# A depthwise-separable convolution on one core: short chunks that share a ring buffer at both ends, and a last supertile in two column parts

## The chip, the cores and the metric

The kernel runs on one core of one Trainium2 chip. The metric is the device time in microseconds (us) of one execution; smaller is better. An execution of some 580 us shows a profiled span of about 578: the profile's span is 1.7 to 2.0 us shorter than the time told for the same run. PE is the matrix engine, PEld its weight loads, DVE the vector engine, ACT the scalar engine, POOL the GpSimd engine and SP the engine that issues nearly all DMA here. A transfer's *landing* is the time from its issue to the last update of its semaphore. For the last store the trace has 16 of these updates, one for each of the 16 DMA engines' shares, and a tiny packet of 4 bytes at the end of each share. A run can start its main loop up to 1.7 us earlier or later, whatever the kernel, as is shown below; differences of a few tenths are therefore read from stretches inside the profiles and not from the times.

## The reference, cut to what matters

```python
# x: (1, 384, 384, 384) bf16, dw: (1, 1, 384), pw: (384, 384)
out = x * dw[0, 0]                         # rewritten: what its padding and loop come to for k = 1
return jnp.einsum('bhwc,cd->bhwd', out, pw)
```

With a 1x1 depthwise kernel the whole is one matrix product: 147,456 rows of 384 channels times a 384x384 weight that has `dw` folded in. Each byte of `x` is read once and each byte of the output written once, 113 MB either way.

## The kernel before

Rows are worked on in **supertiles** of 512. There are 288 of them, numbered 0 to 287. DVE transposes a supertile into `T`, PE multiplies it with the built weight `w_r` into one of two PSUM tiles, ACT empties PSUM into the output buffer `O` (an *eviction*), and SP loads and stores. Loads and stores move **chunks** of up to 10 supertiles, through three buffers of `X` and three of `O`. The chunks are short at both ends, so that the first work starts early and the last store is small.

```python
LMAX = 10
NX = 3
NO = 3

def _chunks(n_super: int):
    head, tail = [1, 1, 2, 2, 3, 4, 5], [7, 5, 4, 2, 1, 1]
    mid = n_super - sum(head) - sum(tail)
    return head + [LMAX] * (mid // LMAX) + tail
# ... cut
        def load_x(t):                       # one chunk, one whole buffer of the ring
            L = chunks[t]
            r = 512 * s0[t]
            src = xf[r : r + 512 * L, :].rearrange("(p s) c -> p (s c)", p=P)
            d = nc.sync.dma_start(Xs[t % NX][:, : 4 * L, :].rearrange("p s c -> p (s c)"), src)
            if t >= NX:
                je = s0[t - NX] + chunks[t - NX] - 1
                d._wait_ge(s_t[je % 2][1], je // 2 + 1)
            d.then_inc(s_x[t % NX], 16)
# ... cut: PE's warm-up matmuls on zeros and the building of w_r
        with nc.tensor.Fori(0, NS // 2, 1) as it:      # all 288 supertiles, two in a turn
            rv = nc.tensor.to_reg(it + 1)
            for s in range(2):
                supertile(s, rv)                       # 48 matmuls of 384 columns
# ... cut
            nq = 4
            if jj + 1 == NS:                           # the last supertile: DVE empties half
                nq = 2
                e = nc.vector.tensor_copy(Ov[:, nq:4, j, :], PS[s][:, nq:4, :D])
                e._wait_ge(s_pe, 2 * jj + 2)
                e.then_inc(s_d)
            a = nc.scalar.copy(Ov[:, 0:nq, j, :], PS[s][:, 0:nq, :D])
            # ... and each of SP and ACT stores its half of the last supertile
```

Of the kernel before, what the change touches and what calls it, by code (L numbers as in the profile page):

```python
# [7 lines left out]
BF16 = mybir.dt.bfloat16  # L8
F32 = mybir.dt.float32
U32 = mybir.dt.uint32  # L10
COPY = mybir.ActivationFunctionType.Copy

LMAX = 10
NX = 3
NO = 3


def _chunks(n_super: int):

    head, tail = [1, 1, 2, 2, 3, 4, 5], [7, 5, 4, 2, 1, 1]  # L20
    mid = n_super - sum(head) - sum(tail)
    assert mid > 0 and mid % LMAX == 0
    return head + [LMAX] * (mid // LMAX) + tail


@with_exitstack
def kernel(
# [4 lines left out]
    pw: bass.AP,  # L32
    out: bass.AP,
):




    nc = tc.nc
    P = nc.NUM_PARTITIONS  # L40
    B, H, W, C = x.shape
    assert dw.shape[0] == 1 and dw.shape[1] == 1, "only k=1 depthwise supported"
    D = pw.shape[1]
    N = B * H * W
    assert C == 384 and D == 384 and N % 1024 == 0
    NB = C // 64

    xf = x.rearrange("b h w c -> (b h w) c")
    of = out.rearrange("b h w d -> (b h w) d")

    NS = N // 512
    chunks = _chunks(NS)
    NT = len(chunks)
    s0 = [sum(chunks[:t]) for t in range(NT)]

    consts = ctx.enter_context(tc.tile_pool(name="consts", bufs=1))
    bufp = ctx.enter_context(tc.tile_pool(name="bufs", bufs=1))
# [6 lines left out]
    w_r = consts.tile([P, NB, 2, D], BF16, name="w_r")  # L64
# [2 lines left out]
    warm = consts.tile([P, 3], F32, name="warm")  # L67
    zero = consts.tile([P, D], BF16, name="zero")

    Xs = [bufp.tile([P, 4 * LMAX, C], BF16, name=f"X{i}") for i in range(NX)]  # L70
    Ts = [bufp.tile([P, NB, 256], BF16, name=f"T{i}") for i in range(2)]
    Os = [bufp.tile([P, 4 * LMAX * D], BF16, name=f"O{i}") for i in range(NO)]
    PS = [psum.tile([P, 4, 512], F32, name=f"ps{s}") for s in range(2)]

    s_x = [nc.alloc_semaphore(f"s_x{i}") for i in range(NX)]
    s_t = [[nc.alloc_semaphore(f"s_t{i}{h}") for h in range(2)] for i in range(2)]
    s_pe = nc.alloc_semaphore("s_pe")
    s_a = [nc.alloc_semaphore(f"s_a{i}") for i in range(2)]
    s_d = nc.alloc_semaphore("s_d")
    s_o = [nc.alloc_semaphore(f"s_o{i}") for i in range(NO)]  # L80
    s_dw = nc.alloc_semaphore("s_dw")
    s_pw = nc.alloc_semaphore("s_pw")
    s_df = nc.alloc_semaphore("s_df")
# [3 lines left out]
    s_wr = [nc.alloc_semaphore(f"s_wr{e}") for e in range(2)]  # L87
    s_seed = nc.alloc_semaphore("s_seed")
    s_zero = nc.alloc_semaphore("s_zero")
    s_last = nc.alloc_semaphore("s_last")  # L90

    with tc.tile_critical():  # L92
        def load_x(t):
            L = chunks[t]
            r = 512 * s0[t]
            src = xf[r : r + 512 * L, :].rearrange("(p s) c -> p (s c)", p=P)
            d = nc.sync.dma_start(Xs[t % NX][:, : 4 * L, :].rearrange("p s c -> p (s c)"), src)
            if t >= NX:
                je = s0[t - NX] + chunks[t - NX] - 1
                d._wait_ge(s_t[je % 2][1], je // 2 + 1)  # L100
            d.then_inc(s_x[t % NX], 16)

        def store(t):
            L = chunks[t]
            r = 512 * s0[t]
            je = s0[t] + L - 1
            dst = of[r : r + 512 * L, :].rearrange("(q p j) d -> p q (j d)", q=4, p=P)
            src = Os[t % NO][:, : 4 * L * D].rearrange("p (q e) -> p q e", q=4)
            nc.sync.wait_ge(s_a[je % 2], je // 2 + 2)
            nc.sync.dma_start(dst, src).then_inc(s_o[t % NO], 16)  # L110


        nc.scalar.dma_start(dw_n[:], dw.rearrange("a e (k p) -> p (a e k)", p=P)).then_inc(s_dw, 16)
        nc.sync.dma_start(pw_n[:], pw.rearrange("(k p) d -> p k d", p=P)).then_inc(s_pw, 16)
        for t in range(NX):
            load_x(t)
        for t in range(NT - 1):
            if t + NX < NT:
                load_x(t + NX)
            store(t)  # L120
        o_last = Os[(NT - 1) % NO][:, : 4 * D].rearrange("p (q e) -> p q e", q=4)
        of_last = of[N - 512 :, :].rearrange("(q p) d -> p q d", p=P)
        nc.sync.dma_start(of_last[:, 2:4], o_last[:, 2:4])._wait_ge(s_d, 1).then_inc(
            s_last, 16
        )
        for o in range(NO):
            nc.sync.wait_ge(s_o[o], 16 * len(range(o, NT - 1, NO)))
        nc.sync.wait_ge(s_last, 32)



# [8 lines left out]
        def supertile(s, rv):  # L140
            for b in range(NB):
                for par in range(2):
                    for q in range(4):
                        if par == 0 and q == 0 and b in (0, 3):
                            nc.tensor.wait_ge(s_t[s][b // 3], rv)
                        mm = nc.tensor.matmul(  # L146
                            PS[s][:, q, :D],
                            lhsT=Ts[s][32 * q : 32 * q + 32, b, par::2],
                            rhs=w_r[32 * q : 32 * q + 32, b, par, :],
                            start=(b == 0 and par == 0),  # L150
                            stop=(b == NB - 1 and par == 1),
                            tile_position=(32 * q, 0),
                        )
                        if b == 0 and par == 0 and q == 0:
                            mm._wait_ge(s_a[s], rv)
                        elif s == 0 and q == 0 and par == 0:
                            mm._wait_ge(*w_done[b])
                        if b in (2, 5) and par == 1 and q == 3:
                            mm.then_inc(s_pe)
# [3 lines left out]
        with nc.tensor.Fori(0, 6, 1) as _:  # L163
            for i in range(8):
                nc.tensor.matmul(  # L165
                    PS[0][:, i % 4, :D],
                    lhsT=zero[32 * (i % 4) : 32 * (i % 4) + 32, 0:P],
                    rhs=zero[32 * (i % 4) : 32 * (i % 4) + 32, :],
                    start=True,
                    stop=True,  # L170
                    tile_position=(32 * (i % 4), 0),
                )
        nc.tensor.wait_ge(s_sel, 1)
        for b in range(NB):
# [4 lines left out]
            for r in range(2):  # L179
                mm = nc.tensor.matmul(  # L180
                    PS[1][:, 2 * (b % 2) + r, :D],
                    lhsT=sel[:, 2 * (b % 2) + r, :],
                    rhs=w_n[:, b // 2, :],
                    start=True,
                    stop=True,
                )
            mm.then_inc(s_w)
        nc.tensor.wait_ge(*w_done[0])
        with nc.tensor.Fori(0, NS // 2, 1) as it:
            rv = nc.tensor.to_reg(it + 1)  # L190
            for s in range(2):
                supertile(s, rv)


        nc.gpsimd.memset(warm[:], 0.0).then_inc(s_seed)  # L195
# [11 lines left out]
        for s in range(2):  # L207
            c = nc.scalar.copy(warm[:, s + 1 : s + 2], warm[:, 0:1])  # L208
# [2 lines left out]
            c.then_inc(s_a[s])  # L211

        def transposes(t, j):
            jj = s0[t] + j
            L = chunks[t]
            s = jj % 2
            Xw = Xs[t % NX][:].bitcast(U32)[:, : 4 * L, :].rearrange("p (k l) c -> p k l c", l=L)
            Tw = Ts[s][:].bitcast(U32).rearrange("p b (i k) -> p b k i", k=4)
            for h in range(2):
                if h == 0 and j == 0:  # L220
                    nc.vector.wait_ge(s_x[t % NX], 16 * (t // NX + 1))
                ins = nc.vector.transpose(  # L222
                    out=Tw[:, 3 * h : 3 * h + 3],
                    in_=Xw[:, :, j, 96 * h : 96 * h + 96].rearrange("p k (b w) -> p b k w", w=32),
                )
                if jj >= 2:
                    ins._wait_ge(s_pe, 2 * (jj - 2) + h + 1)
                ins.then_inc(s_t[s][h])

        order = [(t, j) for t in range(NT) for j in range(chunks[t])]  # L230

        def w_out(b):
            e = w_eng[b]
# [9 lines left out]
        for k in (0, 2):  # L243
            i = nc.vector.tensor_scalar_mul(w_n[:, k, :], pw_n[:, k, :], dw_f[:, k : k + 1])  # L244
            i._wait_ge(s_df, 1)
            i.then_inc(s_wn[k])
        i = nc.scalar.activation(w_n[:, 1, :], pw_n[:, 1, :], COPY, scale=dw_f[:, 1:2])  # L247
        i._wait_ge(s_df, 1)
        i.then_inc(s_wn[1])
        transposes(*order[0])  # L250
        for b in range(NB):
            w_out(b)
        transposes(*order[1])

        for jj, (t, j) in enumerate(order):
            L = chunks[t]
            s = jj % 2
            Ov = Os[t % NO][:, : 4 * L * D].rearrange("p (q j d) -> p q j d", q=4, d=D)
            if j == 0 and t >= NO:
                nc.scalar.wait_ge(s_o[t % NO], 16 * (t // NO))  # L260
            nq = 4
            if jj + 1 == NS:
                nq = 2
                nc.vector.wait_ge(s_o[t % NO], 16 * (t // NO))
                e = nc.vector.tensor_copy(Ov[:, nq:4, j, :], PS[s][:, nq:4, :D])  # L265
                e._wait_ge(s_pe, 2 * jj + 2)
                e.then_inc(s_d)
            a = nc.scalar.copy(Ov[:, 0:nq, j, :], PS[s][:, 0:nq, :D])  # L268
            a._wait_ge(s_pe, 2 * jj + 2)
            a.then_inc(s_a[s])  # L270
            if jj + 2 < NS:
                transposes(*order[jj + 2])
        nc.scalar.dma_start(of_last[:, 0:2], o_last[:, 0:2])._wait_ge(s_a[(NS - 1) % 2], (NS - 1) // 2 + 2).then_inc(
            s_last, 16
        )


# [28 lines left out]
```

## Time and profile before

| | before |
|---|---|
| time, median of 4 runs | 579.64 us (579.41 to 579.90) |
| span of the profiled run | 577.7 us |
| first matmul of the main loop | 10.28 us |
| eviction of supertile 286 begins | 570.44 us |
| issue of the last store, and its landing | 573.37 us, 3.0 us later |

The first 3 of those runs, which the prediction was made from, have a median of 579.63 us. How to read it: between the first matmul and the eviction of supertile 286 lies the loop, 287 supertiles of 1.95 us bound by PE. What lies before it is the head, what lies after it the tail, 7.3 us from the eviction of supertile 286 to the end of the span. That eviction is a good place to cut, because nothing that the change does to the last supertile comes before it. The lines themselves stand in the prediction.

### The profile page before, as it was taken

To read this page: it belongs to the slowest core of one execution; us is meant where nothing else is said; L and a number is where in the kernel's file an instruction comes from. 1 tells how busy PE (TensorE), PEld (TensorE's weight loads), DVE (VectorE), ACT (ScalarE), POOL (GpSimd) and SP (SyncE) were. 2 spreads that over 40 slices of the span, in tenths; PEclk is the share of its full clock that TensorE was granted. 3 is DMA by queue.
4 is the path that set the end of the run, shared out by engine and by line. 5 is a ranking of instruction groups with operands and counts; after the bars stand their busy time and mean duration, and the time that the engine had idled before them with its cause. 6 is when DMAs were issued, how large, how long until landed. Compare 5 with 4: busy or idle time off the path is not lost.

```text
span 577.7 us, 29746 instructions
## 1 busy us (share of the span) xinstructions
PE 569.2 (99%) x13884; PEld 417.2 (72%) x13884; DVE 505.0 (87%) x581; ACT 419.4 (73%) x297; POOL 1.7 (0%) x8
## 2 busy tenths in 40 slices
PE   7999999999999999999999999999999999999996
PEld 3677777777777777777777777777777777777774
DVE  5788898888988889988889888898888898888984
ACT  4777777777777777777777777777777777777775
POOL 1000000000000000000000000000000000000000
PEclk9999999999999999999999999999999999999999
DMA  5999999999999999999999999999999999997987
GB/s 185 360 415 420 430 425 428 438 423 414 426 430 440 405 390 403 423 397 395 402 424 393 395 419 408 397 403 420 406 376 400 426 400 389 397 359 272 367 338 270
DMA packets 26362, 226.88 MB, mean 393 GB/s; under 512 B 1648, under 2 KB 5616, under 8 KB 22384
## 3 DMA queue, kind: packets, MB, share of 16 engines
q1 hardware_dynamic: 25680, 226.60, 97.3%
q10 hardware_dynamic: 672, 0.20, 0.1%
q14 instruction: 9, 0.07, 0.0%
q8 instruction: 1, 0.02, 0.0%
HBM read 113.54 MB, written 113.25 MB: 393 GB/s over the span
## 4 chain that ended last, share of the span: by engine, by line
PE 98%; DMA 1%; DVE 0%; issue 0%; ACT 0%; SPq 0%; DVEq 0%
PE ps L146 97%; DMA pw_n<-in_pw_dram 1%; PE ps L180 0%; DVE w_r L235 0%; DVE O L265 0%; ACT w_r L235 0%; DVE w_n L244 0%; SPq L301 0%; DVEq L241 0%; SPq L92 0%
## 5 line engine op out<-in xcount | busy, mean ns | idle before, releaser
L146 PE MATMUL ps<-w_r,T 32*128 32x384 bf16 x13824 | 562.0, 321 | 0.1
L222 DVE STREAM_TRANSPOSE T<-X 128x384 uint32<-128x384 uint32 x576 | 501.6, 875 | 58.8 <-PE ps L146 3.2
L268 ACT CAST O<-ps 128x1536 bf16<-128x1536 f32 x288 | 413.9, 1437 | 148.1 <-PE ps L146 148.1
L146 PEld LDWEIGHTS ps<-w_r,T 32*128 32x128 bf16 x13824 | 414.4, 93 | 147.6 <-issue 0.8
L244 DVE TENSOR_SCALAR w_n<-pw_n,dw_f 128x384 bf16<-128x384 bf16 x2 | 0.6, 318 | 5.6 <-DMA pw_n<-in_pw_dram 5.6
L165 PE MATMUL ps<-zero 32*128 32x384 bf16 x48 | 4.0, 520 | 1.4 <-POOL zero L196 1.4
L180 PE MATMUL ps<-w_n,sel 128*128 128x384 bf16 x12 | 3.3, 389 | 1.6 <-DVE w_n L244 0.6
L235 ACT CAST w_r<-ps 128x768 bf16<-128x768 f32 x4 | 3.1, 800 | 1.9 <-PE ps L180 1.9
L180 PEld LDWEIGHTS ps<-w_n,sel 128*128 128x128 bf16 x12 | 0.9, 106 | 4.3 <-issue 3.5
L165 PEld LDWEIGHTS ps<-zero 32*128 32x128 bf16 x48 | 1.9, 135 | 2.9 <-issue 1.7
L265 DVE CAST O<-ps 128x768 bf16<-128x768 f32 x1 | 1.0, 958 | 3.0 <-PE ps L146 3.0
L235 DVE CAST w_r<-ps 128x768 bf16<-128x768 f32 x2 | 1.9, 957 | 1.0 <-PE ps L180 1.0
L208 ACT ACT_TABLE_LOAD x1 | 1.3, 1283 | 1.5 <-SPq L92 1.5
L240 ACT CAST dw_f<-dw_n 128x3 f32<-128x3 bf16 x1 | 0.2, 192 | 2.0 <-DMA dw_n<-in_dw_dram 2.0
L247 ACT ACTIVATE w_n<-pw_n,dw_f 128x384 bf16<-128x384 bf16 x1 | 0.6, 615 | 0.4 <-DMA pw_n<-in_pw_dram 0.4
L198 POOL TENSOR_SCALAR_AFFINE_SELECT sel<-ones 128x512 bf16<-128x512 bf16 x1 | 0.7, 737 | 0.1
L197 POOL MEMSET ones<- 128x512 bf16 x1 | 0.5, 531 | 0.0
L208 ACT COPY warm<-warm 128x1 f32<-128x1 f32 x2 | 0.3, 188 | 0.0
L196 POOL MEMSET zero<- 128x192 uint32 x1 | 0.3, 258 | 0.0
L195 POOL MEMSET warm<- 128x3 f32 x1 | 0.1, 101 | 0.5 <-SPq L92 0.5
L290 POOL MEMSET const-bfloat16-1.0<- 128x1 bf16 x1 | 0.1, 102 | 0.0
L290 POOL MEMSET const-uint8-127<- 128x1 uint8 x1 | 0.1, 102 | 0.0
(2 smaller groups left out, 0.2 us busy)
## 6 DMA issues: line engine op xcount, KB each, us to landing
X<-in_x_dram SPq DMA_DIRECT2D x25, 3840.0 KB, 21.8
out_dram<-O SPq DMA_DIRECT2D x25, 3840.0 KB, 27.7
X<-in_x_dram SPq DMA_DIRECT2D x2, 1920.0 KB, 14.1
out_dram<-O SPq DMA_DIRECT2D x2, 1920.0 KB, 18.0
X<-in_x_dram SPq DMA_DIRECT2D x2, 1536.0 KB, 9.9
out_dram<-O SPq DMA_DIRECT2D x2, 1536.0 KB, 14.4
X<-in_x_dram SPq DMA_DIRECT2D x1, 2688.0 KB, 20.1
out_dram<-O SPq DMA_DIRECT2D x1, 2688.0 KB, 11.9
```

The costliest lines, as they stand in the source:

```text
L146: mm = nc.tensor.matmul(PS[s][:, q, :D], lhsT=Ts[s][32 * q : 32 * q + 32, b, par::2], rhs=w_r[32 * q : 32 * q + 32, b, par, :], start=(b = ...
L165: nc.tensor.matmul(PS[0][:, i % 4, :D], lhsT=zero[32 * (i % 4) : 32 * (i % 4) + 32, 0:P], rhs=zero[32 * (i % 4) : 32 * (i % 4) + 32, :], s ...
L180: mm = nc.tensor.matmul(PS[1][:, 2 * (b % 2) + r, :D], lhsT=sel[:, 2 * (b % 2) + r, :], rhs=w_n[:, b // 2, :], start=True, stop=True,)
L197: nc.gpsimd.memset(ones[:], 1.0).then_inc(s_seed)
L198: nc.gpsimd.affine_select(out=sel[:].rearrange("p (v r) (q w) -> p v r q w", v=2, q=4), in_=ones[:].rearrange("p (v r) (q w) -> p v r q w" ...
L208: c = nc.scalar.copy(warm[:, s + 1 : s + 2], warm[:, 0:1])
L222: ins = nc.vector.transpose(out=Tw[:, 3 * h : 3 * h + 3], in_=Xw[:, :, j, 96 * h : 96 * h + 96].rearrange("p k (b w) -> p b k w", w=32),)
L235: i = nc.vector.tensor_copy(out, in_) if e == 0 else nc.scalar.copy(out, in_)
L244: i = nc.vector.tensor_scalar_mul(w_n[:, k, :], pw_n[:, k, :], dw_f[:, k : k + 1])
L247: i = nc.scalar.activation(w_n[:, 1, :], pw_n[:, 1, :], COPY, scale=dw_f[:, 1:2])
L265: e = nc.vector.tensor_copy(Ov[:, nq:4, j, :], PS[s][:, nq:4, :D])
L268: a = nc.scalar.copy(Ov[:, 0:nq, j, :], PS[s][:, 0:nq, :D])
```

## The change

Its intent is at the two ends. **Head:** the chunks 1, 1, 2, 2, 4 lie one after another in one buffer of the ring, each with its own semaphore, so that all of them and two chunks of 10 can be loaded at once. **Tail:** chunks 6, 4 share one buffer and 3, 2, 1, 1, 1 another. **Last supertile:** PE does columns 0 to 255 into one PSUM tile and columns 256 to 383 into the other, so that DVE and ACT can empty the first part beside the matmuls of the second. For that the last two supertiles are written out behind the loop. **Last store:** rows are dealt to partitions so that the store is one run of 3072 bytes per partition, from one issue.

```diff
-    head, tail = [1, 1, 2, 2, 3, 4, 5], [7, 5, 4, 2, 1, 1]
+    head, tail = [[1, 1, 2, 2, 4]], [[6, 4], [3, 2, 1, 1, 1]]
 # ... cut: semaphores per chunk within a buffer, bookkeeping of groups
+            if t + 1 < NT:
+                src = xf[512 * first : 512 * (first + L), :].rearrange("(p s) c -> p (s c)", p=P)
+                dst = dst.rearrange("p s c -> p (s c)")
+            else:
+                src = xf[512 * first :, :].rearrange("(a k q) c -> q a k c", k=4, q=4)
 # ... cut
+                dst = of[512 * first :, :].rearrange("(m q) d -> m (q d)", q=4)
+                nc.sync.wait_ge(s_a[1], NS // 2 + 2)
+                nc.sync.wait_ge(s_d, 3)
 # ... cut: the two half stores of before go
-        with nc.tensor.Fori(0, NS // 2, 1) as it:
+        with nc.tensor.Fori(0, NS // 2 - 1, 1) as it:
             rv = nc.tensor.to_reg(it + 1)
             for s in range(2):
                 supertile(s, rv)
+        supertile(0, NS // 2)
+        for ps, c0, c1 in ((1, 0, DS), (0, DS, D)):        # DS = 256
+            for b in range(NB):
+                for par in range(2):
+                    for q in range(4):
+                        # ... cut: waits, then 48 matmuls of c1 - c0 columns a part
+            mm.then_inc(s_pe)
 # ... cut
+            if jj + 2 < NS:
+                parts = [(s, 0, D, 4, 2 * jj + 2)]
+            elif jj + 2 == NS:
+                parts = [(s, 0, D, 2, 2 * jj + 2)]          # 286: half each by ACT and DVE
+            else:
+                parts = [(1, 0, DS, 2, 2 * jj + 1), (0, DS, D, 2, 2 * jj + 2)]
```

> **What bounds the kernel now.** I read the page first. Matmul is busy for the whole span, and the chain that ended last is 97% the main loop's matmuls:
>
> ```profile
> PE 569.2 (99%) x13884; PEld 417.2 (72%) x13884; DVE 505.0 (87%) x581; ACT 419.4 (73%) x297; POOL 1.7 (0%) x8
> PE 98%; DMA 1%; DVE 0%; issue 0%; ACT 0%; SPq 0%; DVEq 0%
> L146 PE MATMUL ps<-w_r,T 32*128 32x384 bf16 x13824 | 562.0, 321 | 0.1
> L222 DVE STREAM_TRANSPOSE T<-X 128x384 uint32<-128x384 uint32 x576 | 501.6, 875 | 58.8 <-PE ps L146 3.2
> L268 ACT CAST O<-ps 128x1536 bf16<-128x1536 f32 x288 | 413.9, 1437 | 148.1 <-PE ps L146 148.1
> ```
>
> The third line is the reading: 13,824 matmuls cover 562.0 us with 0.1 us idle before them. ACT only waits for PE. In the timeline ACT's evictions of supertiles 7 and 287 start at 26.39 and 572.39 us, so the period is 546.00 / 280 = 1.950 us per supertile of 48 matmuls. The change doesn't touch that loop for the 287 supertiles before the last, so it can only move the two ends. The head, from the timelines of ACT and DVE:
>
> ```profile
> 20.26 1.44 ACT L268 CAST O<-ps 128x1536 bf16<-128x1536 f32 x1 [0.51 <-PE ps L146]
> 22.21 1.44 ACT L268 CAST O<-ps 128x1536 bf16<-128x1536 f32 x1 [0.51 <-PE ps L146]
> 24.44 1.44 ACT L268 CAST O<-ps 128x1536 bf16<-128x1536 f32 x1 [0.79 <-PE ps L146]
> 21.24 4.37 DVE L222 STREAM_TRANSPOSE T<-X 128x384 uint32<-128x384 uint32 x6 [2.06 <-PE ps L146]
> ```
>
> Evictions follow each other by 1.95 us, but 22.21 to 24.44 is 2.23: **one stall of 0.28 us** at supertile 6. DVE sat idle until 21.24. The page puts that on PE, but supertile 6 opens the 3-long chunk, whose load was issued at 14.37 and took 6.8 us: 21.2. It was a load. It was issued late because each small chunk holds a whole ring buffer, so it had to wait until an earlier chunk was transposed. The tail (timeline, then the stretches of the DMA engines, then the landing times):
>
> ```profile
> 572.39 0.80 ACT L268 CAST O<-ps 128x768 bf16<-128x768 f32 x1 [0.51 <-PE ps L146]
> 572.39 0.96 DVE L265 CAST O<-ps 128x768 bf16<-128x768 f32 x1 [3.02 <-PE ps L146]
> 573.22 0.46 ACTq L273 DMA_DIRECT2D out_dram<-O  x1
> 573.37 0.37 SPq L123 DMA_DIRECT2D out_dram<-O  x1
> ```
> ```profile
> 571.00:572.40 1.40, 1.34 (x36) 0.72 (x24) 0.01 (x1) 0.89 (x2) 0.00 (x0) 1.00 1.03 374
> 572.40:573.40 1.00, 0.00 (x0) 0.00 (x0) 0.94 (x1) 0.79 (x1) 0.00 (x0) 1.00 1.03 345
> 573.40:574.40 1.00, 0.00 (x0) 0.00 (x0) 0.00 (x0) 0.00 (x0) 0.00 (x0) 1.00 1.03 311
> 574.40:575.40 1.00, 0.00 (x0) 0.00 (x0) 0.00 (x0) 0.00 (x0) 0.00 (x0) 1.00 1.04 324
> 575.40:576.20 0.80, 0.00 (x0) 0.00 (x0) 0.00 (x0) 0.00 (x0) 0.00 (x0) 1.00 0.33 105
> ```
> ```profile
> out_dram<-O ACTq DMA_DIRECT2D x1, 192.0 KB, 2.7
> out_dram<-O SPq DMA_DIRECT2D x1, 192.0 KB, 3.0
> ```
>
> After PE's last matmul: DVE's half eviction (0.96 us; ACT's is shorter), the SP store issued at 573.37, landed 3.0 us later at 576.4, then 1.3 us of ending to 577.7. The last two columns of the stretches (DMA share, GB/s) show the DMA engines full from 571 to 575.4 us: the last stores stand behind earlier stores.
>
> **What the Trainium skill says.**
> 1. "TensorE: Matmul & The Clock Gate", Back-to-back issue gap: N / 2.4 + 2.5 ns between warm matmuls of N columns. The trace agrees if four 32-row matmuls count as one round: 384 / 2.4 + 2.5 = 162.5 ns, twelve rounds 1.950 us, exactly the period. The same section gives about 81 ns per matmul in streams of weight load and matmul at N = 128, above the formula's 56. This trace has no such narrow matmul in a row group.
> 2. "DMA: Bandwidth & Descriptors", Issuing engines are not separate DMA queues: transfers from SP and ACT run on the same 16 engines. The trace agrees: the two last stores, issued 0.15 us apart, land at nearly the same time.
> 3. The same page, Why a DMA increments its semaphore by 16 and not by 1: the outermost dimension sets how many engines a DMA uses. The new last load has a source whose outermost size is 4, so it may use 4 engines. No view of before shows such a load.
> 4. "Runtime: NRT & Kernel Launch", Instruction fetch mechanics: a taken branch out of the fetched window costs a fetch. Leaving the loop falls through, so I expect none; before ends PE's work at the loop and can't show it.
>
> **The change part by part.**
> - *Head.* Chunks 1, 1, 2, 2, 4 share buffer 0 and are loaded at once, with the two first 10-long chunks behind them. Supertiles 6 to 9 no longer wait for a buffer: ten supertiles are 3.84 MB, about 10 us at 400 GB/s, there well before 20 us. The order in the queue is kept, and the chain to the first main matmul (weights landed at 5.5, w_r built, 10.28 us) has no big load before it. Removes the stall: **-0.28 us**.
> - *Middle.* The same 10-long chunks, same three buffers; order of instructions on ACT unchanged. 0.
> - *Last supertile on PE.* 48 matmuls of 384 columns (1.95 us) become 48 of 256 and 48 of 128. First part 12 x (256 / 2.4 + 2.5 = 109 ns) = 1.31 us. Second part 12 rounds at 56 ns (formula) to 100 ns; I choose 81: 0.97 us. PE ends about 0.33 us later, less about 0.1 since a 128-wide last matmul is itself shorter: **+0.22 us** (from -0.08 to +0.45).
> - *Evictions.* ACT's two sizes (1439 ns for 1536 elements, 800 for 768) give 0.83 ns per element and 160 fixed. With the same fixed part DVE has 1.04 per element: 512 elements 0.69 us, 256 elements 0.43 us. The 512 part runs beside the second matmul part: it starts some 1.5 us after the supertile begins and ends at 2.2, second part's matmuls at 2.4. So what remains after the last matmul is 0.43 in place of 0.96: **-0.53 us**, of which some 0.2 is lost if the matmuls are at the fast end, since DVE is then still at the first part. The two terms together are -0.3; I take **-0.1**, allowing for the wait for PS0 that opens the second part (needs 286's eviction, 0.96 us, within the 1.31 of part one) and for semaphore time between the two evictions.
> - *Store.* Two stores of 256 runs of 768 B become one of 128 runs of 3072 B. ACT's 192 KB took 2.7 us, of which the 384 KB of both at 324 GB/s are 1.2: 1.5 fixed. At the middle's 400 GB/s 384 KB take 1.0: 2.5 in place of 3.0. Nothing should queue ahead: the tail stores of 1152, 768, 384, 384 KB are spread at 1.95 us per 384 KB, which 330 GB/s moves in 1.2, and all loads are done long before the end (issued by about 512 us in place of 561.59). **-0.5 us**.
> - Sum: -0.28 - 0.1 - 0.5 = **-0.9 us**. 579.63 - 0.9 = 578.75, told as 578.8.
>
> **The rivals.**
> - *PE becomes slower at the end.* 96 weight loads in place of 48 for one supertile, and narrow matmuls may be held by them. For it: PEld is busy 72% even at 384 columns (each load shows 93 ns). Against: loads of four row groups overlap. If both parts ran at 162 ns a round, the supertile would take 3.9 us: tail +1.9, less the eviction's and store's gain of 1.0; with the head's 0.28 the time is about 580.3.
> - *A fetch stall leaving the loop*, 144 further matmuls after it: +1 to +2 us, 580 to 581. Against it: PE's stream is short and fetched in order.
> - *The store's landing is fixed latency.* Then only the queue wait goes: -0.2 in place of -0.5, 579.1.
> - *The head's stall is hidden anyway, or the deeper loads delay the first stores.* The first stores now stand behind 11.8 MB of loads, landing near 31 us. ACT first needs that output buffer again at supertile 30, about 69 us, so it costs nothing. Should DMA contention slow the weights' arrival, the head gives back a few tenths.
> - *The middle gains or loses from DMA.* DMA runs at a share of 1.0 and 401 to 425 GB/s in the middle, against a need of 2 x 393 KB per 1.95 us = 403. It is nearly a second bound. But loads are issued some 39 us ahead and land in 21.8, before and after alike, so PE has no wait to lose there.
>
> **Range and chances.** The sure parts (head, absence of the backlog) give -0.5; the unsure are the narrow matmuls (0.5 wide) and the store (0.3 wide). Runs of before lie within 0.24 us. So 578.1 to 579.7. The whole sum is 0.15% of the time and even the worst rival is 0.3%: within 2% almost surely.
>
> **What would show it.** ACT's evictions should show no gap over 1.95 us between 20 and 30 us. The first main matmul should stay at 10.28. All matmuls should end near 572.3. The 128-column rounds should stand at 56 to 100 ns; 160 would be the first rival, a gap before the unrolled part the second. The last DVE eviction should take 0.43 us and the last store 2.5 us to landing, with the DMA share below 1 just before it. The prediction is wrong if PE is idle anywhere in the middle, if the last matmul ends after 573, or if the last store still takes 3 us.

## The result, and the profile after

| | before | after |
|---|---|---|
| time, median of 4 runs | 579.64 us (579.41 to 579.90) | 579.75 us (579.10 to 579.91) |
| span of the profiled run | 577.7 us | 577.4 us |
| eviction of 286 to the end of the span | 7.3 us | 7.6 us |

The ratio is 1.000, with a 95% interval of 0.9982 to 1.0017: the same. Ratios here are the mean time of one kernel's fast runs over that of the other's fast runs of the same rounds, so they are not quite the ratio of the medians quoted. The verdict is the one predicted; the expected gain of 0.9 us is not there, and the median lies 0.05 us above the upper end of the range.

**The page after.** The main loop still has no idle time before it, and the written-out part (its own line, 96 matmuls) has none either:

```profile
L157 PE MATMUL ps<-w_r,T 32*128 32x384 bf16 x13776 | 559.8, 321 | 0.0
...
L217 PE MATMUL ps<-w_r,T 32*128 32x256 bf16 (+1 forms) x96 | 2.2, 241 | 0.0
```

**The head.** In ACT's timeline after the change, the evictions follow each other by 1.95 us through the place where the stall of 0.28 us was:

```profile
19.86 1.44 ACT L306 CAST O<-ps 128x1536 bf16<-128x1536 f32 x1 [0.51 <-PE ps L157]
21.82 1.44 ACT L306 CAST O<-ps 128x1536 bf16<-128x1536 f32 x1 [0.51 <-PE ps L157]
23.77 1.44 ACT L306 CAST O<-ps 128x1536 bf16<-128x1536 f32 x1 [0.51 <-PE ps L157]
25.71 1.44 ACT L306 CAST O<-ps 128x1536 bf16<-128x1536 f32 x1 [0.51 <-PE ps L157]
```

**The tail's compute.** The timeline after 569 us: 286 is evicted from 569.76, the matmuls of both column parts take 2.18 us together, and DVE is done with its two evictions at 571.07 + 1.12 = 572.19, which is 2.43 us after 286's eviction began. Before, that was 1.95 + 0.96 = 2.91 us.

```profile
569.54 2.18 PE L217 MATMUL ps<-w_r,T 32*128 32x256 bf16 x96
...
569.76 0.80 ACT L306 CAST O<-ps 128x768 bf16<-128x768 f32 x1 [0.51 <-PE ps L157]
569.76 0.96 DVE L303 CAST O<-ps 128x768 bf16<-128x768 f32 x1 [1.07 <-PE ps L157]
571.07 1.12 DVE L303 CAST O<-ps 128x512 bf16<-128x512 f32 x2 [0.35 <-PE ps L217]
571.07 1.07 ACT L306 CAST O<-ps 128x512 bf16<-128x512 f32 x2 [0.51 <-PE ps L217]
```

**The tail's store.** The last store is issued at 572.3 us, and the issues' view of the stretch from 571.8 to 573.4 us gives its landing: 3.8 us, where before had 3.0.

```profile
out_dram<-O SPq DMA_DIRECT2D x1, 384.0 KB, 3.8
```

The stretches of the tail are the same five that the prediction shows of before. The last two columns are the DMA engines' share and GB/s. Before, the engines were full until 575.4; after, most of them are busy until about 574.2, and then hardly anything moves for a microsecond while the span still waits:

```profile
572.40:573.40 1.00, 0.00 (x0) 0.00 (x0) 0.00 (x0) 0.00 (x0) 0.00 (x0) 1.00 0.85 278
573.40:574.40 1.00, 0.00 (x0) 0.00 (x0) 0.00 (x0) 0.00 (x0) 0.00 (x0) 1.00 0.78 299
574.40:575.40 1.00, 0.00 (x0) 0.00 (x0) 0.00 (x0) 0.00 (x0) 0.00 (x0) 1.00 0.08 31
575.40:576.20 0.80, 0.00 (x0) 0.00 (x0) 0.00 (x0) 0.00 (x0) 0.00 (x0) 0.72 0.02 8
```

The DMA view of 570 to 577.4 us, in 40 slices of 0.185 us, shows who is late. The first line is the busy share in tenths, the second what was moved; below is one of its queues with packets, MB and share:

```profile
DMA  9999999999999999399999411000000000000000
GB/s 274 365 341 328 324 328 332 328 228 217 303 352 286 303 307 282 108 340 382 411 382 407 158 37 58 25 33 17 33 33 0 0 0 0 0 0 0 0 0 0
...
q8 instruction: 1, 0.02, 1.3%
```

After the 158 come seven slices of 17 to 58. A slice at 17 GB/s is 17 x 0.185 = 3.1 KB, one run of the last store; all 16 engines together move some 400, so 25 belong to one engine. **The last 1.3 us are two engines at work for the first half microsecond and then one, with the others idle.** The third line is new at this place: a packet of instructions of 16 KB, which takes 1.3% of 16 engines for 7.4 us, that is 1.5 us of one engine. In the trace it ran from 571.83 to 573.33. On the whole page that queue has one packet before and two after:

```profile
q8 instruction: 2, 0.03, 0.0%
```

Summed, from the two profiles:

| stretch | before | after | difference |
|---|---|---|---|
| start to the first main matmul | 10.28 | 9.88 | -0.40 (not of the change, as far as seen; see e4 below) |
| from an eviction near 20 us to that of 286 | 550.18 | 549.90 | -0.28 |
| from 286's eviction to the last store's issue | 2.93 | 2.5 | -0.4 |
| the last store's landing | 3.0 | 3.8 | +0.8 |

That is -0.3, as the spans say. Without the first row it is +0.1, which happens to be the difference of the medians too, though they resolve nothing so small. So what was won in the head and in the last supertile was given back in one place, the landing of the last store.

### The profile page after: what moved, and what is told of

It reads as the page before. It is cut to its first block, busy times and chain, and to the rows that moved or that the text cites. A ratio compares the mean times of both kernels' runs of the same rounds, so it can differ in the third digit from the quotient of the medians.

```text
span 577.4 us, 29834 instructions
## 1 busy us (share of the span) xinstructions
PE 568.5 (98%) x13932; PEld 356.0 (62%) x13932; DVE 509.4 (88%) x583; ACT 418.9 (73%) x298; POOL 1.7 (0%) x8
## 3 DMA queue, kind: packets, MB, share of 16 engines
q1 hardware_dynamic: 25924, 226.79, 97.9%
## 4 chain that ended last, share of the span: by engine, by line
PE 97%; DMA 1%; DVE 1%; issue 0%; SPq 0%
PE ps L157 97%; DMA X<-in_x_dram 1%; DVE T L255 0%; PE ps L217 0%; DVE O L303 0%; DVE w_r L268 0%; PE ps L191 0%; SPq L130 0%; SPq L336 0%; SPq L98 0%
## 5 line engine op out<-in xcount | busy, mean ns | idle before, releaser
L157 PEld LDWEIGHTS ps<-w_r,T 32*128 32x128 bf16 x13776 | 351.4, 93 | 208.4 <-issue 0.3
L303 DVE CAST O<-ps 128x768 bf16<-128x768 f32 (+2 forms) x3 | 2.1, 692 | 1.4 <-PE ps L157 1.1
L217 PE MATMUL ps<-w_r,T 32*128 32x256 bf16 (+1 forms) x96 | 2.2, 241 | 0.0
L217 PEld LDWEIGHTS ps<-w_r,T 32*128 32x128 bf16 x96 | 1.9, 93 | 0.3
```

The lines of the kernel that those rows point to most:

```text
L157: mm = nc.tensor.matmul(PS[s][:, q, :D], lhsT=Ts[s][32 * q : 32 * q + 32, b, par::2], rhs=w_r[32 * q : 32 * q + 32, b, par, :], start=(b = ...
L217: mm = nc.tensor.matmul(PS[ps][:, q, : c1 - c0], lhsT=Ts[1][32 * q : 32 * q + 32, b, par::2], rhs=w_r[32 * q : 32 * q + 32, b, par, c0:c1] ...
L303: e = nc.vector.tensor_copy(Ov[:, nq:4, j, c0:c1], PS[ps][:, nq:4, : c1 - c0])
```

## The experiments

Theories (A and B stood ahead of the first set):

- **A, the fetch.** PE's program is longer by the 144 matmuls behind the loop. A further block of 16 KB must be fetched near the end, and its one packet holds one of the 16 DMA engines for 1.0 to 1.9 us. The last store's share on that engine is late, and a store has landed only when its last share has.
- **B, the layout.** One run of 3072 bytes per partition is itself slower to land.
- **C, the parts.** Ahead of the second set it read: the narrow matmuls of the column parts make the last store late. The spacing as its reason was formed after that set: some engine is behind anyway from the saturated middle, and the column parts bring the last two stores closer together (1.46 us apart against 1.94 in e1), so that it cannot catch up.

Three sets ran on three chips, each with its own runs of before. Every run that has a state is a fast one; e6, e6b and e8 are single looks, whose state is unknown.

### First set: one part of the change at a time

**e1_one_part** leaves the last supertile whole and in the loop; everything else of the change stays, the one-run store too.

```diff
-        with nc.tensor.Fori(0, NS // 2 - 1, 1) as it:
+        with nc.tensor.Fori(0, NS // 2, 1) as it:
-        supertile(0, NS // 2)
-        for ps, c0, c1 in ((1, 0, DS), (0, DS, D)):   # ... and its matmuls
 # ... cut: SP waits for one eviction fewer
-                parts = [(1, 0, DS, 2, 2 * jj + 1), (0, DS, D, 2, 2 * jj + 2)]
+                parts = [(1, 0, D, 2, 2 * jj + 2)]
```

> The changed kernel with its last supertile undivided (one part of 384 columns inside the loop, as before), everything else kept, also the store of one run per partition. Theory A (the longer matmul program makes PE fetch a third 16 KB block of instructions near the end, and that one packet holds one of the 16 DMA engines for 1.5 us, so the last store lands late): the 16 KB instruction packets fall from 2 to 1, none in the last 5 us, the last store lands in 2.3 to 2.6 us in place of 3.8, although its eviction takes 0.96 us again (+0.4 us): 1.0 us faster than the changed kernel, about 578.7 us. Theory B (the new store layout or the last load over few DMA engines makes the last store slow): the store still takes 3.7 us or more and the time is 0.4 us longer than the changed kernel's.

Measured: 579.02 us (before of these rounds 580.65), ratio 0.9977 (0.9952 to 1.0001), profiled span 576.7. The first lines are its landing (571.8 to 573.4 us) and then the DMA view from 570 to 576.7 us, in slices of 0.1675 us:

```profile
out_dram<-O SPq DMA_DIRECT2D x1, 384.0 KB, 2.3
```
```profile
DMA  9989999999986999999710079899920000000000
GB/s 358 330 275 413 321 335 330 330 326 335 298 193 193 361 321 303 326 303 330 230 32 23 23 266 459 348 385 440 385 74 0 0 0 0 0 0 0 0 0 0
```

The same store lands in 2.3 us and ends sharply, 385 to 74 to 0. **B falls.** Two things have changed beside the after kernel: no 16 KB packet, and a gap of three slices at 32, 23, 23 GB/s, again one engine's rate, in which the late engine works off what it owes before the last store comes. A is still possible, and so is C, which was put later.

**e3_head_only** keeps the grouped buffers at the head alone, with the tail's chunks in buffers of their own, and before's last supertile and two half stores.

```diff
-    head, tail = [[1, 1, 2, 2, 4]], [[6, 4], [3, 2, 1, 1, 1]]
+    head, tail = [[1, 1, 2, 2, 4]], [[6], [5], [3], [2], [1], [1]]
 # ... cut: the last load, the loop, the evictions and the two half stores are as before
```

> The head's part of the change alone: small chunks of the head share one buffer; tail chunks each with their own buffer, last supertile and its two stores as in the kernel before. Expected by all theories: no gap over 1.95 us between evictions near 22 us, so 0.28 us faster than before at equal clock phase (the matmul clock rises at a time that differs from run to run, which moves the first main matmul by up to 0.4 us either way); the end as before, stores landing in 2.7 and 3.0 us. If the head gains nothing (rival: the stall was hidden), the time stays at 579.6.

Measured: 580.2 us, ratio 0.9992 (0.9968 to 1.0017), landings of 2.4 and 3.0 us, nearly as before (2.7 and 3.0). ACT's timeline has no gap:

```profile
20.04 1.44 ACT L279 CAST O<-ps 128x1536 bf16<-128x1536 f32 x1 [0.51 <-PE ps L154]
21.99 1.44 ACT L279 CAST O<-ps 128x1536 bf16<-128x1536 f32 x1 [0.51 <-PE ps L154]
23.94 1.44 ACT L279 CAST O<-ps 128x1536 bf16<-128x1536 f32 x1 [0.51 <-PE ps L154]
```

The head's gain comes from the head's grouping; a time resolves no 0.28 us in runs spread over 2.6.

**e2_pad** is the after kernel with PE's 48 warm-up matmuls written out instead of looped, meant to bring the fetch forward.

```diff
-        with nc.tensor.Fori(0, 6, 1) as _:
-            for i in range(8):
+        for i in range(48):
```

> The changed kernel with the 48 warm-up matmuls written out in place of 6 turns of 8: the same work, but some 78 more instructions ahead of the main loop on PE. Theory A: the fetch at the end comes some 80 instructions earlier in the last supertiles, so the 16 KB packet starts 1.0 to 1.5 us earlier relative to the end of the matmuls; the held engine catches up in part, and the last store lands in 2.6 to 3.1 us in place of 3.8: 0.7 to 1.2 us faster than the changed kernel. Theory B: nothing at the end moves, 3.8 us, same time.

Measured: 579.64 us, ratio 0.9989 (0.9962 to 1.0016), landing 3.6. A miss: the packet came only 0.26 us earlier, at 571.57, so the landing says nothing between the theories. Where a written-out instruction puts the fetch was not what I had counted.

**e4_after_again** is the after kernel unchanged, on this chip.

> The changed kernel again, on the same chip as the others, for its end in a second profile. Theory A: again two 16 KB instruction packets, the second within 1 us of 571.8 us, and the last store's landing 3.5 us or more with 15 DMA engines done over 1 us before the last. If the late engine was an accident of one run: a landing of 2.6 us or less.

Measured: 580.23 us, ratio 0.9984 (0.9961 to 1.0006), landing 3.9, the 16 KB packet at 573.12 for 1.7 us. It starts 2.0 us after 286's eviction (571.10), as in the first profile (2.07). The late landing repeats, and the packet keeps its place in the program, though 286's eviction comes 1.3 us later. One expectation was missed: not 15 but 14 engines were done over a microsecond before the last (see the table of the third set). The same kernel also shows where the first row of the sum above comes from. These are the same stretch of the head, first of the after kernel's first profile, then of this one; the third column from the end is PE's granted clock, and `(x50)` and `(x19)` are PE's matmuls:

```profile
8.20:11.60 3.40, 2.88 (x50) 1.36 (x52) 2.73 (x4) 1.60 (x2) 0.00 (x0) 1.00 1.05 441
```
```profile
8.20:11.60 3.40, 3.08 (x19) 0.80 (x22) 2.39 (x4) 1.57 (x3) 0.00 (x0) 0.50 1.06 445
```

One kernel, two executions: full clock against half, and 286's eviction 1.3 us later. Over all profiles the main loop's first matmul comes between 9.9 and 11.5 us. The 0.40 us that the after profile starts earlier look to be of this kind: on the pages the 12 matmuls that build `w_r` take 389 ns each in before, 326 in after and 417 in this run.

### Second set: moving the fetch

**e5n_peel_first_only** writes out supertile 0 ahead of the loop instead of 286 behind it; the divided last supertile stays. **e5_peel_first_pad** also writes out the 48 warm-up matmuls, meant to take the fetch away from the end.

```diff
+        supertile(0, 1)
         with nc.tensor.Fori(0, NS // 2 - 1, 1) as it:
-            rv = nc.tensor.to_reg(it + 1)
-            for s in range(2):
-                supertile(s, rv)
-        supertile(0, NS // 2)
+            supertile(1, nc.tensor.to_reg(it + 1))
+            supertile(0, nc.tensor.to_reg(it + 2))
```

> The same with the warm-up left as a loop of 8 matmuls: the two column parts then stand at the same distance from the program's start as in the changed kernel. Theory A: a 16 KB packet again within 1 us of where the changed kernel has it (about 2.0 us after the first 256-column matmul), last store landing 3.5 us or more. If the order of supertiles is what helps: 2.5 us.

> The changed kernel, both column parts kept, but the odd supertile that the loop can't hold is written out ahead of the loop (supertile 0) and not behind it (286), and the 48 warm-up matmuls are written out. Only some 195 instructions then stand behind the loop, and by theory A ([...]the second such place lies about 50 instructions into the last part in the changed kernel) that place moves into the loop, where it is passed in the first turn. Expected: a second 16 KB instruction packet in the first 20 us, none in the last 10 us; last store lands in 2.3 to 2.5 us as in the undivided version, with the short last eviction kept: the end of the span 1.3 to 1.5 us earlier after the last supertile's first matmul than in the changed kernel, a time about 0.35 us under the undivided version: the fastest of all. Theory C (narrow matmuls in two column parts are themselves what makes the last store late): 3.6 us or more again.

Measured: e5n 581.82 us, ratio 1.0018 (0.9996 to 1.004); packet at 574.35, 2.1 us after 286's eviction, for 1.86 us; landing 4.1, as A expected. e5 581.34 us, ratio 1.0007 (0.9984 to 1.003); the packet was still late (573.76, 1.5 us after the eviction) and the landing 4.1 where 2.3 to 2.5 was expected: a miss of the place of the fetch again, not a test of A.

**e6_pair_written_out** is e1 with the last turn of the loop written out, and **e6b_two_pairs** with the last two turns; both whole, both single looks.

```diff
-        with nc.tensor.Fori(0, NS // 2, 1) as it:
+        with nc.tensor.Fori(0, NS // 2 - 2, 1) as it:          # e6: - 1
+        for p in (1, 0):                                       # e6: one pair
+            for s in range(2):
+                supertile(s, NS // 2 - p)
```

> The undivided version (which landed its last store in 2.3 us) with its last turn of the loop written out behind the loop: the same matmuls and the same store, 200 more instructions. Theory A: two 16 KB packets, the second in the last 6 us; if it starts after 571.5 us the last store lands 0.5 to 1.4 us later than 2.3, if it starts before 571 the engine catches up and the landing stays under 2.7. Theory C (narrow matmuls are to blame): 2.3 us and nothing late whatever the packet does.

> As the last, with two turns of the loop written out: the fetch is passed two supertiles (3.9 us) earlier. Theory A: second 16 KB packet 3 to 4 us earlier than with one turn, the last store lands in 2.3 to 2.6 us although the program is still longer. If the mere length of the program is to blame: as late as with one turn or later.

Measured: e6 has no second packet (A had expected one) and lands in 2.3 us, span 576.7, as e1. e6b has it, at 570.22, which is 2.1 us before 286's eviction, and it lands in 2.4 us, nearly as e1:

```profile
q8 instruction: 2, 0.03, 0.0%
```
```profile
SPq L139 <- DMA out_dram<-O: 2.0, 1, 2.0
```

The first is e6b's page. The second, its SP's waits at the end, is 2.0 us for the last store, the same as in e1; in the after kernel it is

```profile
SPq L139 <- DMA out_dram<-O: 3.4, 1, 3.4
```

So writing matmuls out behind the loop costs nothing by itself, and a fetch with four microseconds to spare does no harm. This agrees with A. It does not exclude C, as no kernel so far had divided parts without the late packet.

### Third set: parts without a late fetch, and a fetch without parts

**e7_split_no_late_fetch** is e5n with 80 written-out warm-up matmuls of 230 columns, so that the fetch falls early. **e8_whole_late_fetch** is e6 with the 48 written-out warm-up matmuls, so that a whole last supertile gets a late fetch.

```diff
-        with nc.tensor.Fori(0, 6, 1) as _:
-            for i in range(8):
+        for i in range(80):          # e7, of 230 columns; e8: 48 of 384
```

> The changed kernel with both column parts, supertile 0 written out ahead of the loop in place of 286 behind it, and the warm-up as 80 matmuls of 230 columns written out (the same 4 us of work, 142 more instructions ahead). The pair written out, which made no second fetch, and the divided versions, which did, put the second place of fetching 8 to 23 instructions into the changed kernel's last part; with 142 instructions more ahead of it, it falls into the loop. Theory A: second 16 KB packet in the first 25 us, none later; last store lands in 2.3 to 2.5 us after its issue with the column parts kept, and the span ends 6.4 to 6.6 us after the first 256-column matmul (changed kernel: 7.85). Theory C (the column parts themselves make one DMA engine late): 3.6 us or more, 7.6 us or more.

> The undivided version with its last turn written out and the warm-up's 48 matmuls written out too (78 more instructions ahead): without these 78 it made no second fetch and landed its last store in 2.3 us. Theory A: now a second 16 KB packet, in the last 6 us, and if it starts at 571.3 us or later the last DMA engine is late by 0.4 to 1.2 us: landing 2.7 to 3.5 us. Theory C: no narrow matmuls, so 2.3 us.

**e9_split_fillers** and **e10_whole_fillers** have the same start: 64 written-out warm-up matmuls of 330 columns, and 8 empty matmuls after each of two steps of the weight's building, meant to keep the clock from dropping. e9 is otherwise as e7 (divided), e10 as e1 (whole); neither has a packet near the end.

```diff
 # ... cut: the warm-up
+            if b in (1, 3):
+                for i in range(8):   # matmuls on zeros into PS[0]
```

> The last but one, with the weights' build kept busy: 64 warm-up matmuls of 330 columns (some 0.4 us longer) and 8 more empty matmuls after the second and the fourth of the six build steps. In the profiles so far the matmul clock was granted in full at 5.7 to 13.5 us, and with it the first main matmul came at 9.9 to 11.3 us: that start explains the spread of the times. Expected: first main matmul at 9.8 to 10.5 us in nearly every run, times of 577.9 to 578.7 us with a spread under 0.8, all of them under both kernels. If the clock does not depend on how busy PE is kept, the spread stays 2 us.

> The undivided version with the same warm-up and fillers. By theory A no second fetch; last eviction 0.96 in place of the parts' 0.43 us at the end: 0.35 to 0.45 us slower than the divided version with fillers, 578.3 to 579.1 us, the same small spread.

Measured, on this one chip: e7 580.57 us, ratio 1.0004 (0.999 to 1.0019), its packet at 23.6 us, landing 3.2. e8 581.36 us (one look), packet 1.0 us after 286's eviction, landing 2.9, as A expected. e9 579.65 us, ratio 0.9989 (0.9975 to 1.0003), landing 3.6; its expected time and spread were missed. e10 578.81 us, ratio 0.9965 (0.9951 to 0.9978), landing 2.9; its time is in the expected range, though it was expected to be slower than e9, and its spread of 0.76 us is the smallest of these. The DMA view of e7's end (570 to 578.3 us, slices of 0.2075 us), then of e10's (570 to 577.4 us, 0.185 us):

```profile
GB/s 400 363 385 363 355 370 370 303 355 330 337 318 337 333 278 122 318 329 333 343 318 222 226 422 392 392 403 89 15 30 30 0 0 0 0 0 0 0 0 0
```
```profile
GB/s 357 365 274 382 332 340 320 336 336 320 249 137 328 332 328 324 368 303 104 12 4 208 386 390 419 394 332 33 33 17 17 0 0 0 0 0 0 0 0 0
```

What follows: with the packet gone, the divided kernel lands in 3.2 and 3.6 us, not in 2.3. **A is not the whole cause.** Both views still end in 0.6 to 0.7 us at one engine's rate, with no packet of instructions there. Counted from the issue of 286's store to the last landing, which leaves the spacing out, e1, e6 and e6b needed 4.3 us, e7 4.6, e8 and e10 4.8 to 4.9, e9 5.0 and the after kernel 5.2. By this count e7 and e9 hardly differ from e10, which fits the spacing.

The kept traces say more than the landings do, because they hold the time of each of the 16 semaphore updates. At the end two engines can be late, and they can be told apart. The *trailing* engine is behind in all these kernels, and from the end of its share before, its share of 286's store takes about 1.6 us; the other late engine needs 1.1 or 1.4. The *packet's* engine starts its next share within 0.02 us of the packet's end (after, e4, e5n), ends it 1.05 us after (e2, e5), or had its share done just as the packet began (e8). From the issue of the last store, in us:

| last supertile | run | 16 KB packet | other engines | trailing engine | packet's engine |
|---|---|---|---|---|---|
| divided | after | 2.1 us after 286's eviction | 2.34 | 2.85 | 3.76 |
| divided | e2 (first chip) | 1.8 us after | 2.35 | 2.98 | 3.64 |
| divided | e4 (first chip) | 2.0 us after | 2.33 | 3.11 | 3.89 |
| divided | e5 (second chip) | 1.5 us after | 2.62 | 4.05 | 3.39 |
| divided | e5n (second chip) | 2.1 us after | 2.34 | 3.68 | 4.15 |
| divided | e7, e9 (third chip) | not near the end | 2.35, 2.35 | 3.15, 3.56 | none |
| whole | e1 (first), e6 (second chip) | none | 2.3 | at most 2.33 | none |
| whole | e6b (second chip) | 2.1 us before | 2.3 | 2.38 | in time |
| whole | e8 (third chip) | 1.0 us after | 2.32 | 2.38 | 2.88 |
| whole | e10 (third chip) | none | 2.32 | 2.94 | none |

So A holds for a part of the loss. In the after kernel the packet's engine lands 0.9 us after the trailing one, and in e8, which has no column parts, it alone is late, by 0.5 us. C holds for the other part: on each chip the trailing engine lands later in the divided kernels than in the whole ones, though on the third by as little as 0.2 us, and e10 shows it late with neither parts nor packet. e8 and e10 land alike for different reasons, and in e5 it was the trailing engine that was last and not the packet's. Each row is one profile.

**The version to keep** is e10, the change with a whole last supertile and the fillers. It is the only one whose interval lies below 1. How much of its 0.35% comes from the steadier start and how much from the tail is not separated. e9 (ratio 0.9989) does not separate it: with supertile 0 ahead of the loop, its evictions of supertiles 1 and 2 lie 2.59 us apart in place of 1.95, a stall of 0.64 us that e10 does not have (e7 has one of 0.25). Its cause was not looked for.

## Why the prediction was right or wrong

The verdict, within 2%, was right for the reason given: PE's loop is 97% of the span, and the change touches the ends.

- **Head, -0.28: right.** Measured -0.28 over the loop; e3 shows it with the head's grouping alone.
- **Middle, 0: right.** PE's idle time before the loop's matmuls is 0.0 us.
- **"The two terms taken together are -0.3; I take -0.1": mis-sized, on the safe side.** From 286's eviction to the last store's issue the time fell by 0.4 us (2.93 to 2.5). The rounds of 128 columns were at the fast end, 56 ns in the trace and not the chosen 81, and those of 256 columns 109 as worked out. As feared there, DVE was still at the first part: its two evictions stand back to back, 0.69 and 0.42 us.
- **"Store ... -0.5 us": the step that failed.** It measured +0.8 us: the landing took 3.8 us where 2.5 was forecast, and so the prediction's own last sign of being wrong came ("if the last store still takes 3 us"). Its premise was "Nothing should queue ahead", worked out from the mean rate of all 16 engines. For 14 of the 16 that was right: their shares landed in 2.3 us. But a store lands with its slowest engine; the trailing engine needed 2.9 us and the packet's 3.8. The reasoning took the 16 engines for one pipe.
- **The rivals.** The first, PE slower at the end, did not come: 2.18 us for both parts. The second came in another form. "Leaving the loop falls through, so I expect none" spoke of PE waiting; PE waited 0.0 us for the written-out part. The fetch was there all the same, and its cost fell on the DMA engine that carried it. The third, a fixed latency of the landing, falls with e1: 2.3 us for the same store. The fourth, a head's stall that was hidden anyway, falls with the -0.28. A slip that changes nothing: ten supertiles are 3.93 MB, not 3.84.
- **The last load over four engines.** As suspected from its outermost size of 4, in the trace its 512 packets of 768 bytes run from 522.5 to 529.3 us, mostly at 75 to 100 per us, and its semaphore gets 5 updates where each other load's gets 16: one soon after the issue and four as it lands, from 528.5 to 529.9. It landed well over 30 us ahead of need. Whether it leaves an engine further behind is open. In the store that most engines finish near 557 to 559 us, the last engine trails the other 15 in every kernel: by 3.1 and 3.3 us in before and e3, which have neither this load nor the grouped tail, and by 4.6 to 5.8 in the twelve that have both. No run separates the two.

**What is shown.** The two gains are shown. That the loss lies in the landing, and in the late shares of two engines, is shown by the views and the updates. That both causes are real is shown by the runs: the packet delays its engine in a whole kernel too (e8, against e6 and e6b), and the divided last supertile leaves the trailing engine later on each chip (least clearly on the third). In the after kernel the landing exceeds that of the 14 by 1.4 us; the trailing engine accounts for 0.5 of it, and the packet's engine adds 0.9. **What is argued:** the engines are told apart by times alone, since the trace does not number them, and that the trailing engine cannot catch up because the last two stores come 0.5 us closer together (1.46 us against 1.94, where its two shares took 1.6 and 0.95) is worked out and not tested. **What is open:** why one engine trails at all, and more in some runs than in others.

## What to carry to other kernels

A store at the end lands with the slowest of its engines, so before shortening what comes ahead of it, look in finer slices whether the last microsecond is all engines or one or two, and whether the mean rate hides a straggler. Work written out behind a loop can bring an instruction fetch that costs its own engine nothing and a DMA engine more than a microsecond; with a few microseconds to spare it was harmless. Gains of tenths of a microsecond should be read stretch by stretch, since the same kernel's start varied by more than the whole change was worth.

## What the Trainium skill lacked or had wrong

- "Runtime: NRT & Kernel Launch", Instruction fetch mechanics, calls the cost of crossing a 16 KB block "mostly hidden". For PE that held (0.0 us idle before the written-out matmuls). The page does not say that the block can hold up data: here its packet took 1.0 to 1.9 us of one DMA engine, and in the after kernel that engine's share of the last store landed 0.9 us after any other.
- "DMA: Bandwidth & Descriptors", Latency and other measured facts, has two engines that are usually slower and puts it down to software descriptor generation, as a best guess. Here the data ran on the hardware queue (97.9% of 16 engines' span), and one engine still trailed the other 15, by 3.1 us (before) to 5.8 us (e5) at the store near 557 to 559 us. The trace does not number the engines, so whether it is one of those two stays open.
- "TensorE: Matmul & The Clock Gate", Back-to-back issue gap, gives about 81 ns for 128-column matmuls in streams with weight loads, against 56 by its formula. With four 32-row matmuls side by side, each with its own weight load, a round of four took 56 ns here.
